# Two additions of a Trainium2 transformer block moved to accumulating DMAs on GpSimd

## The chip, the cores and the metric

The kernel runs on one core of one Trainium2 chip. The core has five engines that work side by side: TensorE (PE, matrix products into PSUM), VectorE (DVE), ScalarE (ACT), GpSimd (POOL) and SyncE (SP), which here only issues DMAs. The metric is the device time of one execution in microseconds. The kernel before took 204.91 us in the median of three runs (204.67 to 206.53).

## The reference

One block of a transformer with 2048 positions of 512 features, in bf16: a layer norm with a condition's scale and shift, local attention with 32 heads over 8 positions (every second one, back to 14 positions before), a residual; then a second layer norm with scale and shift, and an MLP that mixes positions (not features), behind a layer norm of its own.

```python
mod = (_silu(c) @ w_mod).reshape(c.shape[0], 6, 1, -1)
sa, ca, ga, sb, cb, gb = (mod[:, i] for i in range(6))
h = _layernorm(x) * (1 + ca) + sa
x = x + ga * _A_ref(h, A_wqkv, A_wo)            # attention over s, s-2, ..., s-14
h = _layernorm(x) * (1 + cb) + sb
x = x + gb * _B_ref(h, B_w1, B_b1, B_w2, B_b2)
...
def _B_ref(x, w1, b1, w2, b2):                   # mixes the 2048 positions
    h = _layernorm(x)
    u = _gelu(jnp.einsum('bsd,sf->bdf', h, w1) + b1)
    return jnp.einsum('bdf,fs->bds', u, w2).transpose(0, 2, 1) + b2
```

Where a line above shortens the original, it keeps what is computed: the shift row that this document speaks of is `sb`, the scale row is `1 + cb`, and the residual is the first `x + ga * ...`.

## The kernel before

The 2048 positions are 16 tiles of 128 positions by 512 features. `xx` holds them all in SBUF. Attention runs over five chunks of 2, 4, 4, 4 and 2 tiles (`SIZES`). For each chunk there are these steps, by the names that the order uses (the numbers behind a name are the chunk and a part, or the tile):

- `ln1s`, `ln1v`, `rstd1`, `nb1`, `n1`: statistics and normalisation of the input tile, into `h3`. Statistics may be taken by VectorE (`:d`, two instructions) or by ScalarE (`:a`, two passes with an accumulator, and then a small VectorE column `ln1v`).
- `tr`/`hT` or `xt`: the transpose, by TensorE or by a DMA. `qkv` and `ev`: the projections and their evictions from PSUM.
- `qk`: VectorE multiplies q with k shifted by 0 to 14 positions, four instructions of 128x4096 per chunk (128x2048 for the short first and last chunk); `red`: TensorE adds up the heads' features into `psL`.
- `max`, `sub`, `exp`, `esum`, `rcp`, `smB`: the softmax.
- `vd` and `a2`: DMAs that lay out v and the weights; `pv`: VectorE's products of both; `pvacc`, `oev`: their sums and eviction.
- `wo`: the output projection of a tile, four matmuls and a fifth of `xx` with the identity that adds the residual in PSUM; `x1`: ScalarE evicts the sum into `xx` and collects its mean. For tiles 14 and 15 VectorE adds the residual in `x1` itself (`:d`), and the fifth matmul is left out.
- `ln2q` (ScalarE, sum of squares), `ln2m`, `rstd2`, `nb2`, `n2`: the second norm, into `h2`. `aff`: VectorE multiplies by the scale row and adds the shift row, two instructions over one, two or four tiles (`GRP`).
- `ln3s`, `ln3v`, `rstd3`, `nb3`, `h3`: the MLP's norm of `h2`, into `h3`.

The MLP's first product `mlp1` takes tiles of `h3` as they come: a group of its matmuls needs four neighbouring tiles, the first group tiles 0 to 3. Its sums are parked in `gT` (`park`), later ones are added (`padd`) and go through `gelu`. The second product `mlp2` needs all of `gT`; `fin` adds bias and residual and `st_out` stores.

What runs when is written out by hand: the string `ORDER` (L182) lists every step once, and `schedule` (L87) walks it. Each engine executes its own instructions in that order and waits for what they need. A suffix picks the engine or form: `:d` VectorE, `:a` ScalarE, `:p` GpSimd (for `warm`, done on TensorE, where `:s` leaves it out), `:q` a matmul cut into four quarter matmuls of 32 output rows. `warm` are matmuls of the identity whose result nobody reads. All DMAs but one are issued by SP, in the order of the list; each of them waits on SP's queue for what it needs, and those behind it wait with it.

The lines that the change touches are the residual and second norm in `build_chunk` (L798 to L855):

```python
                if res:
                    mm(ps(s_), lhsT=ident[:], rhs=xx[:, st, :], start=False, stop=True)
...
                nc.scalar.activation(xx[:, st, :], ps(s_), ACT.Identity, **acc)
...
        hv = h2[:, g0 - t0:g0 - t0 + gn, :]
        nc.vector.tensor_tensor(hv, hv, ab_bc[:].unsqueeze(1).to_broadcast([P, gn, D]), op=ALU.mult)
        nc.vector.tensor_tensor(hv, hv, sb_bc[:].unsqueeze(1).to_broadcast([P, gn, D]), op=ALU.add)
```

Of the kernel before, what the change touches and what calls it, by code (L numbers as in the profile page):

```python
# [161 lines left out]
def _t_tt2(n):  # L162
    return 0.154 + 0.00052 * n
# [14 lines left out]
def _t_mm(cols, n=1):  # L178
    return n * (cols / 2400.0 + 0.0024)
# [3 lines left out]
ident ld_x0 act_table ld_wmod1 ld_c cps ln1s0:d ln1v0 silu_exp silu_dve ld_x1 ln1s1:d ln1v1 ld_x_1_2 ln1s2:d warm0:p  # L183
rstd1_0 consts halo0 ld_x_1_4 nb1_0 n1_1:p ln1s4:d ld_wmod0 ln1s3:d ln1s5:a ln1v2 ln1v5 ln1v3 ln1v4 ld_x_3_12 rstd1_1
nb1_1 n1_4:d n1_3:a modcols1 modcols0 a1col n1_0:p tr0_0 hT0_2:a hT0_3:a ld_x_2_8 n1_2:p n1_5:d hT0_1:a tr1_2 tr1_0
sab ld_wqkv0 wsc0_3:p qvb0 ln1s8:d ln1s9:a ld_wqkv1 ln1s13:d hT0_0:d qkv0_00 qkv0_10 wsc0_1:p hT1_3:d hT1_1:a hT1_2:d
wsc0_0:p ln1s12:d ln1v9 wsc0_2:a ld_x_2_6 qvb_cp0 ev0_00:a ln1s6:d ev0_10:a qkv0_12 ln1s7:d ln1v12 qkv0_02 hT1_0:a
ln1v6 ln1v8 qkv1_10 ev0_12:a ev0_02:a qk0_1 ev1_10:a ld_wo2 ln1v7 ln1v13 rstd1_2 ld_wqkv2 qvb1 wsc1_0:p wsc1_3:p
ld_x_3_10 wsc2_1:a ld_wmod5 qkv1_00 ev1_00:a qk0_0 qk0_3 ld_wo3 nb1_2 n1_8:a qvb_cp1 qkv0_20 ev0_20:a wsc1_2:a ld_b1
qkv0_22 ev0_22:a ld_x_4_14 red0_0 qk0_2 warm5:s red0_1 red0_2 red0_3 ln1s11:d mask ln1s14:a qkv1_01 qkv1_12 ev1_01:a  # L190
ld_wo0 ln1s10:d wsc2_0:p ld_wmod2 qkv1_11 ev1_11:a ld_wmod4 max0 sub0 exp0 n1_6:p xt6 ev1_12:a qkv1_02 qk1_0 n1_9:a
ld_wmod3 esum0 rcp0 ev1_02:a qkv1_03 ln1v11 ev1_03:a ln1v14 qkv1_13 ld_wo1 qk1_1 n1_7:p ln1v10 smB0 qk1_2 vd0_2 xt7
modrow rstd1_3 xt8 xt9 ev1_13:a nb1_3 a2_0_3 qk1_3 qkv1_22 mrows:a ld_row0 a2_0_1 wsc1_1:a qkv1_21 qkv1_20 ln1s15:a
woq_s a2_0_0 halo_v1:a vd0_0 ev1_20:a wsc2_3:a ln1v15 red1_0 red1_1 red1_2 red1_3 max1 a2_0_2 n1_13:a pv0_2 qkv2_01:q
n1_12:p vd0_1 qkv1_23:q ld_row1 ev1_22:a wsc2_2:a n1_10:a sub1:q vd0_3 xt10 exp1 ev2_01:a pv0_1 qkv2_10:q ev2_10:a
pv0_0 qkv2_11:q pvacc0_2 xt13 pv0_3 esum1 rcp1 smB1 a2_1_3 ev2_11:a qkv2_00 pvacc0_0 qkv2_02:q pvacc0_3 ev1_23:a
ev1_21:a vd1_2 qkv2_03:q qk2_1 a2_1_2 pvacc0_1 vd1_3 oev0_2:a ev2_00:a qkv2_12 halo_v2:a oev0_0:a qk2_0 ev2_02:a wo0
qkv2_13 ev2_12:a qk2_2 qkv2_21 n1_11:a qkv2_22 ev2_13:a a2_1_1 rstd1_4 nb1_4 ev2_03:a qk2_3 xt12 n1_14:a wo1 x1_1:a
red2_0 ln2q1 qkv2_23 ev2_23:a qkv2_20 a2_1_0 xt11 qkv3_01 pv1_2 x1_0:a ln2q0 ln2m0 red2_1 ev2_22:a vd1_0 pv1_0 qkv3_02
red2_2 red2_3 ev3_01:a ev2_20:a ev3_02:a ld_row2 qkv3_11 rstd2_0 ev3_11:a qkv3_13 max2 vd1_1 nb2_0 n2_0:a ev2_21:a  # L200
vd2_3 sub2 xt14 pv1_3 pvacc1_2 exp2 pv1_1 qkv3_10:q qkv3_12:q esum2 n2_1:a ev3_12:a qkv3_00 rcp2 vd2_2 ev3_13:a ld_b2
ev3_00:a oev1_2:a smB2 a2_2_0 pvacc1_1 oev1_1:a pvacc1_3 ld_w1_0_896 oev1_3:a pvacc1_0 qkv3_03 halo_v3:a oev1_0:a wo3
ld_w1_0_512 a2_2_3 wo2 aff0 qk3_2 a2_2_2 ev3_10:a ln3s1:a ln3s0:a qk3_1 ev3_03:a qkv3_23 warm3:s a2_2_1 x1_2:a x1_3:a
ln2q2 ln3v1 ln2q3 ln3v0 qk3_0 warm1:s ev3_23:a vd2_0 wo4 x1_4:a n1_15:p wo5 qkv3_20 biascols ev3_20:a ln2q4 red3_0
x1_5:a pv2_2 xt15 qkv4_00 ln2q5 ln2m2 rstd2_2 rstd3_0 pvacc2_2 qk3_3 nb3_0 ev4_00:a h3_1:a red3_1 qkv4_22 qkv4_12
nb2_2 n2_2:a biascols_cp:a vd2_1 pv2_1 ev4_22:a red3_2 red3_3 n2_3:p oev2_2:a ev4_12:a ln2m4 max3 qkv3_21 warm4:p
warm2:s aff2 qkv3_22 sub3 ev3_21:a exp3 ld_w1_0_0 pv2_0 pv2_3 qkv4_20 h3_0:p ev3_22:a rstd2_4 nb2_4 n2_4:p esum3 rcp3
qkv4_02 ln3s3:d ev4_20:a pvacc2_1 oev2_1:a halo_v4:a pvacc2_0 oev2_0:a n2_5:d ln3s2:a qkv4_10 pvacc2_3 oev2_3:a
ev4_10:a ln3v3 ln3v2 rstd3_2 aff4 nb3_2 smB3 wo7 ev4_02:a h3_3:p wo8 x1_7:a wo9 vd3_3 wo6 ln3s5:d h3_2:a mlp1_0_4_0
mlp1_0_0_0 ld_w2_3 vd3_1 ln3s4:a x1_6:a qk4_1 x1_8:a ln3v5 qk4_0 red4_0 ln3v4 rstd3_4 qk4_3 a2_3_3 a2_3_1 vd3_0  # L210
mlp1_0_2_0:q x1_9:a a2_3_2 red4_1 ln2q9 mlp1_0_3_0:q qk4_2 red4_2 nb3_4 ln2q7 h3_4:a red4_3 a2_3_0 pv3_1 h3_5:a
mlp1_0_1_0:q mlp1_0_1_4:q vd3_2 max4 mlp1_0_0_4:q mlp1_0_3_4:q pvacc3_1 mlp1_0_2_4:q ln2q8 vd4_3 ln2q6 sub4:q
park0_0:a park0_1:a oev3_1:a mlp1_0_4_4:q mlp1_0_6_0:q vd4_0 park0_2:a park0_3:a ld_w1_0_1152 pv3_0 pvacc3_0
mlp1_0_5_0:q exp4 park0_4:a oev3_0:a ln2m6 rstd2_6 pv3_2 mlp1_0_5_4:q park0_5:a nb2_6 n2_6:a n2_9:a pv3_3 mlp1_0_8_0:q
pvacc3_2 ld_w2_4 mlp1_0_7_0:q mlp1_0_9_0:q n2_8:a pvacc3_3 oev3_2:a vd4_1 oev3_3:a n2_7:p mlp1_0_6_4:q esum4
ld_w1_0_1408 aff6 rcp4 park0_6:a smB4 a2_4_1 ln3s7:d wo13 ln3s8:d ln3s9:d ln3v8 ln3s6:d x1_13:a ln2q13 wo10 x1_10:a
ln2q10 wo11 x1_11:a wo12 ln3v7 x1_12:a ln2q12 ln3v9 ln3v6 rstd3_6 nb3_6 a2_4_3 mlp1_0_10_0 mlp1_0_12_0:q a2_4_2 ln2m10
h3_6:d ln2m12 a2_4_0 ld_w2_1 h3_7:a pv4_1 rstd2_10 nb2_10 mlp1_0_11_0:q h3_9:p mlp1_0_12_4:q ln2q11 ln2m11 h3_8:a
n2_10:a pv4_3 ld_row3 rstd2_12 nb2_12 rstd2_11 mlp1_0_8_4:q mlp1_0_7_4:q mlp1_0_7_8:q park0_7:a aff10 mlp1_0_10_4:q
mlp1_0_10_8:q pv4_0 vd4_2 pv4_2 nb2_11 mlp1_0_8_8:q ld_w1_0_1664 ln3s10:a park0_8:a mlp1_0_9_4:q mlp1_0_9_8:q  # L220
ld_w1_1_0 park0_9:a ln2m13 n2_11:p ln3v10 pvacc4_0 pvacc4_1 oev4_0:d mlp1_0_12_8:q pvacc4_2 n2_12:a pvacc4_3 aff12
mlp1_0_11_4 mlp1_0_11_8 aff11 oev4_2:a wo15 x1_15:d rstd2_13 nb2_13 wo14 rstd3_10 nb3_10 mlp1_0_13_0 ld_w1_1_640
x1_14:d ln2s14:d mlp1_0_13_4 h3_10:p ln2v14 n2_13:p aff13 park0_10:a park0_11:a ln3s11:a ln3v11 ln2s15:a rstd2_14
nb2_14 n2_14:p mlp1_0_13_8 ln2v15 ln3s12:d rstd2_15 park0_12:a park0_13:a mlp1_1_0_6 mlp1_1_0_10 mlp1_1_1_6 mlp1_1_4_6
rstd3_11 mlp1_1_4_10 nb2_15 aff14 ln3s14:d ln3v14 mlp1_1_2_6 mlp1_1_2_10 ln3s13:a n2_15:p rstd3_14 nb3_11 ln3v12 aff15
ln3s15:d rstd3_12 nb3_12 ln3v13 rstd3_13 ln3v15 mlp1_1_6_6 nb3_14 mlp1_1_1_10 padd1_0 rstd3_15 mlp1_1_5_6 mlp1_1_5_10
padd1_1 nb3_13 h3_14:p mlp1_1_6_10 mlp1_1_3_6 nb3_15 h3_15:p h3_11:d padd1_2 h3_12:a ld_w1_1_896 mlp1_1_3_10 h3_13:a
mlp1_1_7_10 mlp1_1_10_10 padd1_3 padd1_4 padd1_5 padd1_6 padd1_10 ld_w2_5 mlp1_1_8_10 padd1_8 gelu8 mlp1_1_9_10
padd1_9 gelu9 padd1_7 gelu7 ld_w1_2_0 mlp1_2_1_11 mlp1_2_0_11 mlp1_2_1_14 ld_w2_2 mlp1_2_0_14 padd2_0 gelu0
mlp1_2_2_11 mlp1_2_2_14 padd2_2 gelu2 padd2_1 gelu1 ld_w1_2_640 mlp1_2_3_11 mlp1_2_4_11 mlp1_2_3_14 mlp1_2_4_14  # L230
padd2_3 gelu3 ld_w1_1_1408 mlp1_2_5_11 mlp1_2_5_14 padd2_4 gelu4 padd2_5 gelu5 mlp1_2_6_11 gelu10 padd2_6 gelu6
ld_w2_0 mlp1_1_11_10 padd1_11 mlp1_1_12_10 mlp1_1_13_10 padd1_13 mlp2_0_0 gelu11 mlp2_0_0b ld_w2_15 gelu13 padd1_12
gelu12 mlp2_5_0 ld_w2_7 mlp2_0_0c fin0_0 mlp2_6_0 ld_w2_9 ld_w2_11 mlp2_4_0 mlp2_8_0 st_out0_0 fin4_0 mlp2_2_0
ld_w2_13 st_out4_0 fin8_0 mlp2_1_0 fin1_0 st_out1_0 mlp2_3_0 fin3_0 st_out3_0 fin2_0 st_out8_0 mlp2_7_0 mlp2_12_0
mlp2_9_0 mlp2_13_0 st_out2_0 fin5_0 fin7_0 st_out7_0 fin12_0 st_out5_0 fin6_0 st_out6_0 fin9_0 mlp2_11_0 st_out9_0
fin13_0 fin11_0 st_out11_0 mlp2_10_0 mlp2_14_0 fin10_0 mlp2_15_0 st_out10_0 fin14_0 st_out14_0 fin15_0 st_out13_0
st_out15_0 mlp2_15_1 st_out12_0 fin15_1 mlp2_15_2 fin15_2 st_out15_1 st_out15_2
# [4 lines left out]
def kernel(  # L242
# [15 lines left out]
    NPRE=6,  # L258
    NBIG=4,
    NVD: int = 5,  # L260
    NHT: int = 2,
    NA2: int = 2,
    NB=2,
    NH2=2,
    ESD=(4,),
    LN2D=(14, 15),
    GRP=(2, 2, 4, 1, 1),
    XDMA=(2, 3, 4),
    INJ=(),
    WARM=(48, 24, 16, 16, 8, 8),  # L270
):
    nc = _OrderedNC(tc, 1)
    G = _Graph(dict(ps=6, big=NBIG, vd=NVD))
    CM = max(SIZES) * P
    MT = max(SIZES)
    NCH = len(SIZES)
    T0 = [sum(SIZES[:i]) for i in range(NCH + 1)]

    x_view = A_x[0].rearrange("(t p) d -> p t d", p=P)
    out_flat = out[0]  # L280
    w1_view = B_w1.rearrange("(t p) f -> p t f", p=P)
    w2_view = B_w2.rearrange("(t p) s -> p t s", p=P)
# [722 lines left out]
```

## Time and profile before

| | us |
|---|---|
| three runs, median (lowest to highest) | 204.91 (204.67 to 206.53) |
| the profiled execution, its own time | 205.73 |
| its span, first to last instruction | 203.9 |
| TensorE busy | 190.8 |
| VectorE busy | 159.7 |
| ScalarE busy | 129.6 |
| GpSimd busy | 31.2 |
| mean granted TensorE clock | 0.973 |

The profiled execution's time is 1.83 us longer than its span: what lies before its first and after its last instruction. All operations pass through one recording helper, so every instruction carries its line, L133; they are told apart by the names of the tiles they write and read (`out<-in`). In the lists, a row gives engine, operation, tiles, shape, count, busy time in us and mean ns of one, and after the bar the engine's idle time just before and what ended it. In the timeline, a row begins with start and duration in us, and neighbours of one kind are merged.

Names of tiles: `big` products of q·k and of weights·v, `psS` and `psL` PSUM, `h` any of `h2` and `h3` (buffer numbers are left out), `wst` MLP weights, `rows_bc` the four rows of the condition, spread over the partitions, `mv`, `rs`, `nb`, `sums` columns of the norms.

### The profile page before, as it was taken

Reading aid. Unit: us, or ns where it says so; the run is one execution under the profiler, and the core shown is the slowest. Engines: PE = TensorE matmul, PEld = TensorE weight load, DVE = VectorE, ACT = ScalarE, POOL = GpSimd, SP = SyncE. Lnnn points to the kernel's source line nnn. Section 1 sums busy time; section 2 is a strip of 40 time slices with the busy share of each in tenths; the row PEclk is TensorE's granted clock in tenths of the full one; section 3 lists DMA queues with packets and bytes.
Section 4 is the critical chain, followed back from the end, with each engine's and each line's share of the span. In section 5 each row is a group of like instructions: output and inputs, shape, how many; then the busy total and the mean of one; then the engine's idle time right before and its main releaser. Section 6 shows DMA issues by size and latency. Waiting matters only on the chain.

```text
span 203.9 us, 4231 instructions
## 1 busy us (share of the span) xinstructions
PE 190.8 (94%) x1643; PEld 99.2 (49%) x1643; DVE 159.7 (78%) x244; ACT 129.6 (64%) x311; POOL 31.2 (15%) x50
## 2 busy tenths in 40 slices
PE   5389999999999979989999999999999999999993
PEld 5377654454344436634454464444444444444453
DVE  2687999999999989999999898996741241696554
ACT  2396999987979999899999999873642000000000
POOL 4263403100500006030040103330000000000000
PEclk9856999999999999999999999999999999999999
DMA  5999686649727993267495647789999340022013
GB/s 167 340 325 296 191 199 128 213 55 264 197 80 247 270 309 103 92 197 230 166 264 141 141 121 226 200 249 221 240 297 281 97 136 3 26 97 83 0 55 105
DMA packets 55369, 35.94 MB, mean 176 GB/s; under 512 B 24628, under 2 KB 52788, under 8 KB 55348
## 3 DMA queue, kind: packets, MB, share of 16 engines
q1 hardware_dynamic: 55340, 35.66, 63.3%
q8 instruction: 13, 0.21, 0.5%
q14 instruction: 8, 0.07, 0.1%
q10 hardware_dynamic: 8, 0.00, 0.0%
HBM read 22.03 MB, written 2.10 MB: 118 GB/s over the span
## 4 chain that ended last, share of the span: by engine, by line
PE 60%; DVE 18%; DMA 8%; ACT 5%; SPq 5%; issue 2%; POOL 0%; DVEq 0%
PE psS L133 58%; DVE big L133 8%; SPq L133 5%; DMA a2sb<-lsb 4%; DVE h L133 3%; DMA xx<-in_A_x_dram 3%; DVE st L133 2%; PE psL L133 2%; DVE m L133 2%; DVE mv L133 1%; DMA rows_bc<-mrows 1%; ACT xx L133 1%; ACT junk L133 1%; DVE lsb L133 1%; ACT q_sb L133 1%
## 5 line engine op out<-in xcount | busy, mean ns | idle before, releaser
L133 PEld LDWEIGHTS <-wst 128*32 128x32 bf16 (+1 forms) x626 | 37.2, 101 | 33.0 <-issue 1.6
L133 PE MATMUL psS<-h,wst 128*32 128x512 bf16 (+1 forms) x476 | 51.3, 379 | 0.1
L133 DVE TENSOR_TENSOR big<-a2sb,vD 128x4096 bf16<-128x4096 bf16 (+1 forms) x20 | 37.0, 1876 | 0.8 <-PE psS L133 0.5
L133 DVE TENSOR_TENSOR big<-q_sb,k_f 128x4096 bf16<-128x4096 bf16 (+1 forms) x20 | 36.6, 1858 | 1.3 <-POOL w_qkv L133 1.0
L133 POOL TENSOR_SCALAR h<-xx,rs,nb 128x512 bf16<-128x512 bf16 x14 | 19.7, 1409 | 85.2 <-DVE nb L133 62.0
L133 PE MATMUL psS<-hT,w_qkv 128*32 128x512 bf16 (+2 forms) x228 | 29.9, 358 | 1.3 <-ACT v_sb L133 1.3
L133 DVE SCALAR_TENSOR_TENSOR h<-psS,bcol,rows_bc 128x512 f32<-128x512 f32 (+2 forms) x18 | 12.4, 691 | 23.5 <-PE psS L133 18.3
L133 PEld LDWEIGHTS <-w_qkv 128*128 128x128 bf16 (+1 forms) x270 | 19.7, 109 | 17.6 <-issue 5.1
L133 PE MATMUL psS<-gT,big 128*128 128x512 bf16 x112 | 25.0, 379 | 0.0
L133 PEld LDWEIGHTS <-big 128*128 128x128 bf16 x144 | 12.0, 98 | 16.5 <-DMA big<-in_w_mod_dram 3.2
L133 PE MATMUL psS<-woq,o_sb 128*128 128x512 bf16 x64 | 16.4, 380 | 0.3 <-ACT o_sb L133 0.3
L133 ACT ACTIVATE junk<-xx 128x512 bf16<-128x512 bf16 x24 | 15.1, 629 | 2.0 <-DMA xx<-in_A_x_dram 1.5
L133 ACT ACTIVATE gT<-psS,bcol 128x512 bf16<-128x512 f32 x14 | 9.1, 687 | 7.9 <-DVE psS L133 7.9
L133 DVE TENSOR_TENSOR psS<-psS,gT 128x512 f32<-128x512 f32 x14 | 9.4, 697 | 5.9 <-PE psS L133 5.9
L133 PE MATMUL psS<-hT,wst 128*128 128x256 bf16 (+1 forms) x64 | 13.3, 372 | 0.0
L133 DVE BATCH_NORM_STATS2 st<-xx 128x6 f32<-128x512 bf16 x13 | 8.9, 681 | 5.4 <-DMA xx<-in_A_x_dram 5.3
L133 ACT ACTIVATE h<-xx,nb,rs 128x512 bf16<-128x512 bf16 x15 | 12.0, 811 | 1.6 <-DVE nb L133 1.5
L133 DVE TENSOR_TENSOR h<-h,rows_bc 128x512 bf16<-128x512 bf16 (+2 forms) x20 | 12.0, 605 | 0.3
L133 ACT ACTIVATE q_sb<-psS,qvb 128x512 bf16<-128x512 f32 (+1 forms) x20 | 11.4, 593 | 1.0 <-PE psS L133 1.0
L133 DVE TENSOR_TENSOR h<-h,xx 128x512 bf16<-128x512 f32 (+2 forms) x18 | 11.4, 633 | 0.7
L133 ACT ACTIVATE v_sb<-psS,qvb 128x512 bf16<-128x512 f32 (+1 forms) x20 | 11.4, 596 | 0.0
L133 PEld LDWEIGHTS <-group 128*32 128x32 bf16 x288 | 6.6, 95 | 9.6 <-issue 3.5
(91 smaller groups left out, 240.4 us busy)
## 6 DMA issues: line engine op xcount, KB each, us to landing
vD<-v_sb SPq DMA_DIRECT2D x12, 524.5 KB, 3.6
big<-in_B_w_dram SPq DMA_DIRECT2D x4, 896.0 KB, 9.1
vD<-v_sb SPq DMA_DIRECT2D x8, 268.5 KB, 2.7
wst<-in_B_w_dram SPq DMA_DIRECT2D x3, 640.0 KB, 4.8
out_dram<-h SPq DMA_DIRECT2D x15, 128.0 KB, 1.7
xx<-in_A_x_dram SPq DMA_DIRECT2D x7, 256.0 KB, 7.0
wst<-in_B_w_dram SPq DMA_DIRECT2D x2, 800.0 KB, 4.7
gT<-in_w_mod_dram SPq DMA_DIRECT2D x3, 512.0 KB, 7.6
```

The source lines that it names most:

```text
L133: r = fn(*a, **k)
```

## The change

Two steps get another way of doing them, and one of these ways is chosen per tile in the order:

- *Residual.* A third form of `wo`/`x1`, suffix `:t`: the identity matmul is left out, ScalarE evicts the projection into the tile's place in `h2`, and a new step `xa` on GpSimd first corrects the sum column by the input's mean and then issues a DMA that adds `h2` to `xx`, SBUF to SBUF. It is chosen for tiles 0, 3 and 10. VectorE adds the residual in `x1` (`:d`) for tiles 13 and 14, where it was 14 and 15.
- *Shift row.* `aff` is cut into `affm` (the multiplication, VectorE) and `affa` (the addition), and `affa` may be a DMA of GpSimd, suffix `:p`, that adds the row to `h2`. It is chosen for `affa0` and `affa4` (two tiles each), `affa11` and `affa12` (one each).

The variance columns `ln2m` are computed with scaled sums (the sign and the division move into ScalarE's logarithm); for a single tile this takes one instruction where there were two. And the whole of `ORDER` is a new list: all steps of the old one are there, but most stand elsewhere, and many have another suffix. For instance, the four `qk4` products and `red4` stand ahead of the first `mlp1`, `h3_0`, `h3_2` and `h3_3` are VectorE's, and 37 steps with `:q` become 18.

```diff
@@ parameters
+    ADDS=(2, 2, 2, 2, 1),
+    RDMA=(1, 1, 1, 1, 0),
@@ ln_rstd
-            nc.scalar.activation(lv[:, sl, 0], var, ACT.Ln, bias=epscol[:, 0:1])
+            nc.scalar.activation(lv[:, sl, 0], var, ACT.Ln, bias=epscol[:, 0:1], scale=1.0 if vreads is None else -1.0 / D ** 2)
@@ build_chunk, residual
+            tmp = h2[:, st - t0, :]
+
+            def fx_t(st=st, s_=s_, acc=acc, tmp=tmp):
+                nc.scalar.activation(tmp, ps(s_), ACT.Identity, **acc)
+
+            def fx_p(st=st, tmp=tmp):
+                nc.gpsimd.tensor_scalar(sums[:, st, 0:1], ln_t["mv", 0][:, st, 0:1], float(D), sums[:, st, 0:1],
+                                        op0=ALU.mult, op1=ALU.add)
+                nc.gpsimd.dma_start(xx[:, st, :], tmp, accum_op=ALU.add)
...
+            x1 = wo_.link = G.add_any([("act", 0.69, fx_a), ("dve", 0.75, fx_d), ("temp", 0.69, fx_t)][:na], frees=s_,
+                      writes=[("xx", st)] + ([] if st in LN2D else [("sum0", st)]) + h2k, name=f"x1_{st}")
+            if na == 3:
+                G.add_any([("dve", 0.0, lambda: None), ("dve", 0.0, lambda: None), ("pool", 1.5, fx_p)], reads=h2k,
+                          writes=[("xx", st), ("sum0", st)], link=x1, name=f"xa{st}")
@@ build_chunk, variance of the second norm
+                    if gn == 1:
+                        nc.vector.scalar_tensor_tensor(mv[:, g0, 1:2], sums[:, g0, 0:1], sums[:, g0, 0:1],
+                                                       sums[:, g0, 1:2], op0=ALU.mult, op1=ALU.subtract)
+                        return
...
@@ build_chunk, scale and shift rows
-                nc.vector.tensor_tensor(hv, hv, ab_bc[:].unsqueeze(1).to_broadcast([P, gn, D]), op=ALU.mult)
-                nc.vector.tensor_tensor(hv, hv, sb_bc[:].unsqueeze(1).to_broadcast([P, gn, D]), op=ALU.add)
...
+            add("dve", _t_tt2(gn * D), lambda hv=hv, bc=bc: nc.vector.tensor_tensor(hv, hv, bc(ab_bc), op=ALU.mult),
+                reads=hk + ["ab_bc"], writes=hk, locks=True, name=f"affm{g0}")
+            G.add_any([("dve", _t_tt2(gn * D), lambda hv=hv, bc=bc: nc.vector.tensor_tensor(hv, hv, bc(sb_bc), op=ALU.add)),
+                       ("pool", 1.3, lambda hv=hv, bc=bc: nc.gpsimd.dma_start(hv, bc(sb_bc), accum_op=ALU.add))][:ADDS[ch]],
+                      reads=hk + ["sb_bc"], writes=hk, locks=True, name=f"affa{g0}")
@@ ORDER, the stretch ahead of the first MLP matmuls
+ev3_20:a affm4 pv2_1 esum3 ln3s1:d n2_2:a ln3v1 n2_3:p halo_v4:a halo_v3:a vd3_0 affa4:p vd3_3 ln3s0:a ln3v0 affm2
+qkv4_10 rcp3 warm3:p rstd3_0 smB3 affa2:d pvacc2_1 qk4_3 pvacc2_3 oev2_3:a ld_w1_0_512 a2_3_3 qkv4_00 oev2_1:a wo6
+ev4_10:a ev4_00:a wo7 qk4_0 ln3s2:a ln3v2 a2_3_1 ln3s4:a wo8 ln3s3:a wo9 qk4_1 red4_0 red4_1 qkv4_20 qk4_2 red4_2
+nb3_0 x1_9:a ln3v3 rstd3_2 red4_3 ln3s5:d ln3v5 nb3_2 ln3v4 h3_0:d h3_2:d h3_1:p x1_8:a xa8 h3_3:d mlp1_0_0_0:q
```

## The prediction

> **What bounds the kernel now.** First the page's busy row, then a table of stages, then the instructions around the place where the stages meet. The page:
>
> ```profile
> PE 190.8 (94%) x1643; PEld 99.2 (49%) x1643; DVE 159.7 (78%) x244; ACT 129.6 (64%) x311; POOL 31.2 (15%) x50
> ```
>
> TensorE looks like the bound, but its busy time counts pipelined matmuls that overlap. The table of stages (columns: stretch, length, busy time and instructions of each engine, granted clock, DMA share, GB/s) gives its pace:
>
> ```profile
> 0.00:18.76 18.76, 12.66 (x142) 11.06 (x143) 11.34 (x36) 9.87 (x24) 9.00 (x33) 0.73 0.94 284
> 18.76:92.90 74.14, 70.49 (x664) 36.70 (x663) 72.32 (x73) 69.14 (x163) 13.20 (x8) 1.00 0.69 182
> ...
> 140.00:190.00 50.00, 50.00 (x233) 22.71 (x232) 25.35 (x37) 9.05 (x14) 0.00 (x0) 1.00 0.50 138
> ```
>
> The last row is the pure MLP: about 232 matmuls of 512 columns in 50 us, 0.2157 us each. I count all matmul columns of the program at that pace (a quarter matmul, 128*32, as a quarter, a floor of 25 ns for tiny ones, warm-ups left out). The kernel needs 176.1 us of TensorE and its span is 203.9, so 27.8 us are lost. The timeline says where:
>
> ```profile
> 92.67 0.38 PE L133 MATMUL psS<-xx,ident 128*128 128x512 bf16 x1
> 92.88 1.89 PE L133 MATMUL psS<-h,wst 128*128 128x512 bf16 x8
> ```
>
> At 92.88 the first MLP matmul starts. Work done by then is 69.7 us, so 23.2 us are already lost. The other 106.4 us take 203.9 - 92.88 = 111.0, so only 4.6 us are lost behind it (3.2 of them after the last matmul). **Before the first MLP matmul TensorE waits for others; after it, it never does.** Who it waits for is in the second row of the table: VectorE is busy 72.32 of 74.14 us, ScalarE 69.14. So two numbers set the time: when the first MLP matmul can start, and how much TensorE work is left then.
>
> **The change, part by part.** The named edits are small. Three tiles (0, 3, 10) lose their identity matmul: 3 x 0.2157 = 0.65 us of TensorE. Their ScalarE eviction stays, at the same 588 ns, into another tile. Four shift-row additions leave VectorE (tiles 0-1 and 4-5 at 688 ns each, 11 and 12 at 460 each): 2.30 us. GpSimd gets three one-column operations and seven DMAs. But the written order is new throughout, and it moves far more than that. Summed over the program by the rows of before, VectorE ends at +0.7 us (171.6 against 170.9 of listed durations, additions moved and all), ScalarE at -0.3, GpSimd loses four tile normalisations. No engine gets lighter by more than 0.7 us; what counts is what stands ahead of the first MLP matmul.
>
> That matmul needs the second normalised input of tiles 0 to 3. Before, VectorE's last instruction for it is the nb column of tiles 2-3:
>
> ```profile
> 18.76 3.55 DVE L133 TENSOR_TENSOR big<-q_sb,k_f 128x2048 bf16<-128x2048 bf16 x3 [0.97 <-POOL w_qkv L133]
> ...
> 90.46 0.15 DVE L133 SCALAR_TENSOR_TENSOR nb<-mv,rs 128x2 f32<-128x2 f32 x1
> ```
>
> From the first q·k product to that column VectorE executes 69 instructions whose rows sum to 74.3 us, in 90.61 - 18.76 = 71.85 us: 0.967 us per listed us, as neighbours overlap a little. After, the stretch runs from the first product to the third normalisation (h3_3 is VectorE's now) and holds 76 instructions, priced by these rows and their like:
>
> ```profile
> L133 DVE TENSOR_TENSOR big<-q_sb,k_f 128x2048 bf16<-128x2048 bf16 x8 | 9.4, 1217 | 1.0 <-POOL w_qkv L133 1.0
> ...
> L133 DVE TENSOR_TENSOR h<-h,rows_bc 128x1024 bf16<-128x1024 bf16 x6 | 4.1, 688 | 0.1
> ...
> L133 DVE TENSOR_SCALAR h<-h,rs,nb 128x512 bf16<-128x512 bf16 x2 | 1.2, 608 | 0.0
> ```
>
> Added: the four products of the last chunk, ahead of it now, 4 x 1.217 = 4.87; three normalisations, 3 x 0.608 = 1.82; four more variance columns, 0.84; one v eviction, 0.69; chunk 3's softmax scaling, 0.69. Gone: two two-tile additions, 1.38; one norm, 0.50; tile statistics, 0.86; small columns, 0.17. Net +6.0, so 80.3 us, times 0.967 = 77.6.
>
> When does VectorE begin? Its first product waits for 24 matmuls of 256 columns. In before 36 of them took 6.59 us (183 ns each, clock 0.56 from 9 to 20 us). The changed order sends 72 warm-ups directly ahead, but puts the first bias columns (0.70), their copy (0.15) and a VectorE eviction (0.69) between. The weights it needs are 2.8 MB down the load queue, as in before (13.8 us). Between 109 ns and 183 ns a matmul this gives 17.9 to 19.7 us; I keep 18.8. So h3_3 ends at 18.8 + 77.6 = 96.4.
>
> ScalarE could hold it up. From 18.8 to the last of its instructions that h3_3 needs, its rows (90.3 - 13.2 = 77.1 listed us before) took 71.3 us with 5.0 idle, so 0.860 busy us per listed one. After, 82.4 listed us stand there, among them three more tile statistics of 1.64: 70.9 us, so it could be done at 89.7, and VectorE asks for it at 94.5. The reserve, 4.8 us, is what it was. The cost is 0 to 1.0 us and I take 0.5. First MLP matmul: **96.9**.
>
> TensorE has then done 70.0 us and 105.4 remain; with the same 4.6 lost behind, the span is 96.9 + 105.4 + 4.6 = 206.9, **+3.0 us**. Fewer quarter matmuls cost nothing by the rows (four take the time of one); six more switches of form at about 0.1 us are inside the rounding. Of the warm-ups, the extra 1.8 us fall where TensorE waits anyway; if that cover is gone, they cost 1.8.
>
> The seven DMAs I cost at nothing, if they land under their cover. No GpSimd DMA is in the trace. Nearest rows: SBUF-to-SBUF copies of 128 and 268 KB land 2.6 and 2.7 us after issue, at worst 5.3; issue takes SP 0.6, and a GpSimd operation beside VectorE's products up to 2.6 (below). So 3.2 to 7.9 us, nearer the first, as most such copies are. What queues behind: ScalarE's square of tile 0 has 7 us of other work between, of tile 3 over 6, of tile 10 only 3.2; VectorE's statistics after the additions have 8, 5.3 and, for tile 11, 3.9; tile 4's, on ScalarE, 9. SP's queue is not passed by them.
>
> The profiled execution took 205.73 us round its span of 203.9. The median, 204.91, is 0.8 lower; +3.0 on it is **207.9 us**.
>
> **The rivals.**
>
> *Not slower: the front starts early.* If 72 warm-ups keep the clock at full, the first product starts at 17.9 (-0.9); if ScalarE costs nothing, -0.5; if the 1.4 us of small gaps behind 92.88 close, up to -1.2 more; and the normalisations, at 0.41 where GpSimd is quiet, -0.6. All together 207.9 - 3.2 = 204.7. For it: clock 0.56 exactly where TensorE sat idle 3.1 us after its warm-ups. Against: VectorE's 80.3 listed us still stand there. It decides once h3_3 ends before 94.
> The Trainium skill, "TensorE: Matmul & The Clock Gate", Part 1, says that the clock opens after some 3.4 us of sustained work and closes again after an idle window; the 0.56 after a 3.1 us gap agrees.
>
> *Slower still: late landings.* GpSimd slows beside VectorE:
>
> ```profile
> 78.32 2.64 POOL L133 TENSOR_SCALAR h<-xx,rs,nb 128x512 bf16<-128x512 bf16 x1 [24.77 <-DVE nb L133]
> 80.95 0.76 POOL L133 TENSOR_SCALAR h<-h,rs,nb 128x512 bf16<-128x512 bf16 x1
> ```
>
> The same work takes 0.76 alone and 2.64 beside a 2.29 us product. If descriptors suffer like this, tile 11's addition lands up to 4.0 us late. VectorE waits in order, with the statistics and norms of tiles 11 to 15 behind it. TensorE needs the last of these at once (136.0 in before), so beyond about 1.5 us it passes on: at 4.0 us, 2.5 more, 210.4.
> The Trainium skill, "SBUF — State Buffer", Who interferes with whom, says that VectorE locks GpSimd out in its two-port modes, copies and tensor_scalar among them, and so starves descriptor writing, while tensor_tensor blocks only GpSimd's reads. By that rule the products would leave the DMAs alone and the sum at 207.9; by the row they may cost up to 2.5 us more. No run here shows it yet.
>
> *The order is neutral.* If the edits alone count and TensorE's losses stay as they are, -0.65: 204.3. For it: engine totals hardly move. Against: the first MLP matmul has no other supplier.
>
> **How the numbers follow.** Forecast 0.52 (own range 206.0 to 210.0), early front 0.20, late landings 0.17, neutral order 0.11. The range 203.5 to 212.0 holds all but the outer parts of the rivals. One per cent, about what a measurement of this kernel can tell from no change, is 202.9 to 207.0. Faster: 0.04 of the early front and 0.06 of the neutral order, 0.10. Within: 0.16 and 0.05 of these and 0.05 of the forecast, 0.26. Slower: the rest, 0.64.
>
> **What would show it.** First psS<-h,wst matmul at about 97 (before 94: the early front); VectorE still above 97% busy from its first product to there; loss behind it still near 4.6; GpSimd DMAs landing within 3 to 5 us, and VectorE idle before st<-h of tile 11 under 1 us. I am wrong if VectorE has finished the four last-chunk products and h3_3 by 93, or if TensorE starves after its first MLP matmul.

## The result and the profile after

| | before | after |
|---|---|---|
| three runs, median (lowest to highest), us | 204.91 (204.67 to 206.53) | 222.62 (220.60 to 223.22) |
| span of the profiled execution, us | 203.9 | 220.6 |
| first q·k product on VectorE, us | 18.76 | 24.71 |
| first MLP matmul, us | 92.88 | 107.36 |
| from there to the end of the span, us | 111.0 | 113.2 |

Medians and ranges, here and below, leave out executions over 1.5% above the fastest of their kernel (two of five of c_first_w512 and five of ten of mix_red0_3).

The kernel became slower: ratio 1.083, 95% interval 1.072 to 1.094. The prediction was 207.9 us, and its range ended at 212.0. Its forecast of the span, 206.9, is missed by 13.7 us, and the three stages share that: the first product is 5.9 us later than the 18.8 I kept, the stretch from it to the first MLP matmul takes 82.65 us instead of 78.1 (4.6 more), and what follows takes 113.24 instead of 110.0 (3.2 more).

The busy row of the page after:

```profile
PE 192.9 (87%) x1474; PEld 98.3 (45%) x1474; DVE 158.4 (72%) x244; ACT 130.2 (59%) x311; POOL 38.8 (18%) x56
```

No engine has lost or gained much work, except GpSimd (31.2 before). So most of the new time is waiting. The table of stages of the changed kernel (stretch, length, busy time and instructions of each engine, granted clock, DMA share, GB/s):

```profile
0.00:24.71 24.71, 12.82 (x177) 12.24 (x177) 11.26 (x38) 13.27 (x32) 7.59 (x32) 1.00 0.83 255
24.71:107.36 82.65, 71.14 (x583) 35.03 (x582) 74.30 (x75) 70.16 (x166) 21.18 (x12) 0.99 0.60 171
```

Before, VectorE was busy 72.32 of 74.14 us in the second stage. Now it is busy 74.30 of 82.65: it is no longer what everybody waits for. The waits say what is. First ScalarE's timeline at the start of the changed kernel (start, duration, engine, line, operation; in brackets the idle time before it and what ended it):

```profile
5.01 0.63 ACT L133 ACTIVATE junk<-xx 128x512 bf16<-128x512 bf16 x1
5.55 0.19 ACT L133 ACTIVATION_READ_ACCUMULATOR junk<-xx 128x1 f32 x1
5.77 0.63 ACT L133 ACTIVATE junk<-xx 128x512 bf16<-128x512 bf16 x1
5.78 0.54 ACTq L133 DMA_DIRECT2D c_t<-in_c_dram  x1
...
11.98 0.17 ACT L133 ACTIVATE ecol<-psS 128x4 f32<-128x4 f32 x1 [5.49 <-PE psS L133]
```

and TensorE's timeline there, with the matmul that waits for it:

```profile
11.77 0.18 PE L133 MATMUL psS<-ident,c_t 4*128 4x4 bf16 x1 [11.77 <-DMA c_t<-in_c_dram]
11.88 6.24 PE L133 MATMUL psS<-ident 128*128 128x128 bf16 x72
```

The load of the condition `c` is the one DMA that ScalarE issues (`ACTq`). In the new list it stands behind two tile statistics of ScalarE (`ln1s3:a`, `ln1s5:a`), which wait for tiles of x. Before, it was issued at 0.83 us and its matmul ran at 2.20:

```profile
0.83 0.54 ACTq L133 DMA_DIRECT2D c_t<-in_c_dram  x1
2.20 0.18 PE L133 MATMUL psS<-ident,c_t 4*128 4x4 bf16 x1 [2.20 <-DMA c_t<-in_c_dram]
```

Now it is issued at 5.78, when the DMA engines are busy with SP's loads (their share is 0.83 in this stage), and it lands 5.94 us after that. TensorE does nothing at all for 11.77 us, ScalarE stands idle 5.49, and VectorE 6.8 behind it. The 72 warm-ups, 6.24 us, stand behind that matmul in TensorE's order, so here they too come only after the load has landed.

Then the place where the stages meet, first in ScalarE's timeline of the changed kernel:

```profile
98.08 0.63 ACT L133 ACTIVATE junk<-h 128x512 bf16<-128x512 bf16 x1
98.61 0.19 ACT L133 ACTIVATION_READ_ACCUMULATOR junk<-h 128x1 f32 x1
102.53 0.63 ACT L133 ACTIVATE junk<-h 128x512 bf16<-128x512 bf16 x1 [3.73 <-DMA h<-rows_bc]
```

In VectorE's timeline:

```profile
105.61 0.22 DVE L133 SCALAR_TENSOR_TENSOR mv<-mv,st 128x1 f32<-128x1 f32 x1 [4.21 <-ACT junk L133]
```

And in TensorE's:

```profile
107.36 1.05 PE L133 MATMUL psS<-h,wst 128*32 128x512 bf16 x8 [4.72 <-ACT lv L133]
```

ScalarE waits 3.73 us for an accumulating DMA: the shift row of tiles 4-5. It wants tile 4's statistics, which the first MLP matmul does not need; but tile 3's, which it does need, stand behind them in ScalarE's order. So VectorE idles 4.21 us and TensorE 4.72. GpSimd's timeline shows when that DMA was issued:

```profile
88.93 5.31 POOL L133 TENSOR_SCALAR h<-xx,rs,nb 128x512 bf16<-128x512 bf16 x1 [7.36 <-DVE nb L133]
94.19 1.20 POOL L133 DMA_DIRECT2D h<-rows_bc  x1
```

VectorE had the tile multiplied at 91.56, but GpSimd was still in a normalisation that took 5.31 us beside VectorE's products, so the DMA went out 2.6 us late. It landed at 102.45, 8.3 us after issue.

Last, what lies behind that, in the table of stages of the changed kernel (the granted clock is the third number from the right):

```profile
108.00:110.00 2.00, 2.00 (x24) 0.86 (x20) 2.00 (x2) 2.00 (x6) 0.77 (x1) 0.50 0.00 0
```

and in VectorE's timeline:

```profile
143.75 0.69 DVE L133 BATCH_NORM_STATS2 st<-h 128x6 f32<-128x512 bf16 x1 [2.90 <-DMA h<-rows_bc]
```

After its idle time TensorE works at a granted clock of 0.50, so part of the wait is paid for a second time (how much, no run isolates); and VectorE waits 2.90 us for the shift row of tile 11, with the statistics and norms of later tiles behind it.

### The profile page after: what moved, and what is told of

It is laid out like the page before. It is cut to its first block, busy times and chain, and to the rows that moved or that the text cites. A ratio compares the mean times of both kernels' runs of the same rounds, so it can differ in the third digit from the quotient of the medians.

```text
span 220.6 us, 3897 instructions
## 1 busy us (share of the span) xinstructions
PE 192.9 (87%) x1474; PEld 98.3 (45%) x1474; DVE 158.4 (72%) x244; ACT 130.2 (59%) x311; POOL 38.8 (18%) x56
## 4 chain that ended last, share of the span: by engine, by line
PE 43%; DVE 21%; DMA 15%; ACT 8%; SPq 6%; issue 6%; DVEq 0%; ACTq 0%
PE psS L133 43%; DVE big L133 13%; DMA h<-rows_bc 7%; SPq L133 6%; DMA a2sb<-lsb 5%; ACT junk L133 3%; DMA c_t<-in_c_dram 3%; DVE h L133 3%; DVE st L133 1%; DMA xx<-in_A_x_dram 1%; ACT h L133 1%; DVE mv L133 1%; DVE m L133 1%; ACT xx L133 1%; DVE lsb L133 1%
## 5 line engine op out<-in xcount | busy, mean ns | idle before, releaser
L133 PE MATMUL psS<-h,wst 128*32 128x512 bf16 (+1 forms) x368 | 53.0, 407 | 5.7 <-ACT lv L133 4.7
L133 PEld LDWEIGHTS <-wst 128*128 128x128 bf16 (+1 forms) x530 | 36.0, 104 | 40.1 <-issue 11.0
L133 DVE TENSOR_TENSOR big<-a2sb,vD 128x4096 bf16<-128x4096 bf16 (+1 forms) x20 | 36.8, 1870 | 3.7 <-DMA a2sb<-lsb 3.7
L133 DVE TENSOR_TENSOR big<-q_sb,k_f 128x4096 bf16<-128x4096 bf16 (+1 forms) x20 | 37.2, 1897 | 0.1
L133 PE MATMUL psS<-hT,w_qkv 128*128 128x512 bf16 (+1 forms) x144 | 29.3, 345 | 0.0
L133 PEld LDWEIGHTS <-w_qkv 128*128 128x128 bf16 x186 | 19.3, 111 | 17.6 <-issue 4.0
L133 DVE SCALAR_TENSOR_TENSOR h<-psS,bcol,rows_bc 128x512 f32<-128x512 f32 (+2 forms) x18 | 12.4, 690 | 18.5 <-PE psS L133 18.1
L133 PE MATMUL psS<-gT,big 128*128 128x512 bf16 x112 | 24.8, 379 | 0.0
L133 POOL TENSOR_SCALAR h<-xx,rs,nb 128x512 bf16<-128x512 bf16 x10 | 12.3, 1238 | 51.3 <-DVE nb L133 38.3
L133 ACT ACTIVATE junk<-xx 128x512 bf16<-128x512 bf16 x30 | 18.9, 629 | 2.3 <-DMA xx<-in_A_x_dram 1.4
L133 PEld LDWEIGHTS <-big 128*128 128x128 bf16 x144 | 12.0, 97 | 13.2
L133 PE MATMUL psS<-woq,o_sb 128*128 128x512 bf16 x64 | 16.3, 380 | 0.7 <-ACT o_sb L133 0.7
L133 DVE TENSOR_TENSOR h<-h,xx 128x512 bf16<-128x512 f32 (+2 forms) x18 | 11.4, 632 | 6.6 <-DMA out_dram<-h 6.2
L133 ACT ACTIVATE h<-xx,nb,rs 128x512 bf16<-128x512 bf16 x20 | 15.7, 811 | 0.4 <-DVE nb L133 0.3
L133 ACT ACTIVATE gT<-psS,bcol 128x512 bf16<-128x512 f32 x14 | 9.0, 685 | 8.4 <-DVE psS L133 8.4
L133 PEld LDWEIGHTS <-group 128*32 128x32 bf16 x288 | 5.9, 95 | 15.9 <-issue 7.9
L133 DVE TENSOR_TENSOR psS<-psS,gT 128x512 f32<-128x512 f32 x14 | 9.3, 695 | 5.2 <-PE psS L133 5.1
L133 PE MATMUL psS<-big,group 128*32 128x512 bf16 (+1 forms) x160 | 9.7, 339 | 3.4 <-DVE big L133 3.4
L133 PE MATMUL psS<-hT,wst 128*128 128x256 bf16 (+2 forms) x76 | 11.7, 336 | 0.1
L133 ACT ACTIVATE q_sb<-psS,qvb 128x512 bf16<-128x512 f32 (+1 forms) x18 | 10.7, 612 | 1.5 <-PE psS L133 1.4
L133 PEld LDWEIGHTS <-ident 128*128 128x128 bf16 (+1 forms) x132 | 10.0, 114 | 3.3 <-issue 1.8
L133 ACT ACTIVATE k_f<-psS 128x512 bf16<-128x512 f32 x16 | 9.3, 591 | 2.2 <-PE psS L133 1.1
```

The source lines that it names most:

```text
L133: r = fn(*a, **k)
```

## The experiments

I had three suspects: the *queue* (the load of `c`), the *landing* (the DMAs of GpSimd land late, above all tiles 4-5) and the *order* (the new list has stalls of its own). The first four kernels take them apart. All share the first edit:

```diff
-... ln1s3:a ld_x_1_4 ln1s4:d ln1s5:a ln1v4 ident ln1v3 ld_x0 ld_c cps
+... act_table ld_c ln1s2:d ... ln1s5:a ln1v4 ident ln1v3 ld_x0 cps
```

**c_first.** The edit above alone.

> Changed kernel with the load of c moved up to stand right behind the first activation of ScalarE, as it did before. Queue theory (c was late because its DMA is issued on ScalarE's queue behind two tile statistics, and lost its place on the DMA engines): first q.k product back from 24.7 to about 18.8, all of it kept, time 222.6 - 5.9 = about 216.7 us (215.5 to 218). Rival (the front is set by the weight loads, or the gain is eaten by the waits behind it): product above 22 or the time above 219.5.

Measured 215.12 us (214.79 to 215.59), 7.5 less than the changed kernel. The first product stands in VectorE's timeline at 17.45:

```profile
17.45 2.36 DVE L133 TENSOR_TENSOR big<-q_sb,k_f 128x2048 bf16<-128x2048 bf16 x2
```

The queue theory holds, and the place of one tiny load was the largest single loss; the gain is 1.6 us more than I expected. The product is even 1.3 us earlier than in the kernel before; the granted clock is 1.00 from 9 to 20 us, where it was 0.56. But the first MLP matmul only comes at 100.4: what followed kept its stalls.

**c_first_add_dve.** The four shift rows go back to VectorE:

```diff
-affa0:p ... affa4:p ... affa11:p ... affa12:p
+affa0:d ... affa4:d ... affa11:d ... affa12:d
```

> As c_first, and the four shift-row additions go back to VectorE. Landing theory (the addition of tiles 4-5 lands 8.3 us after issue and stops ScalarE 3.7 us, that of tile 11 costs some 1.8): 6.4 us gained, 1.3 us of VectorE work put back ahead of the first MLP matmul, about 211.7 us, 5 below c_first. Rival (the DMAs only fill time that VectorE's longer order would take anyway): 216 to 218, no better than c_first.

Measured 209.14 us (208.86 to 210.21): 6.0 less than c_first, though VectorE has 2.3 us more to do. The landing theory had said 5, and holds.

**c_first_res_pe.** The residuals of tiles 0, 3 and 10 go back to TensorE:

```diff
-x1_0:t ... x1_3:t ... x1_10:t
+x1_0:a ... x1_3:a ... x1_10:a
```

> As c_first, and the residuals of tiles 0, 3 and 10 go back to the identity matmul on TensorE; the shift rows stay DMAs. Landing theory (nobody waits for a residual DMA for more than some tenths, and it is the shift rows that land late): within 1 us of c_first, by the matmuls 0.65 longer. Rival (the residual DMAs delay ScalarE's squares, and the shift rows behind them on the same queue): 2 us or more below c_first.

Measured 214.01 us (212.89 to 215.54), 1.1 below c_first, and the runs of the two overlap. ScalarE's two waits for residual DMAs in c_first are 1.1 us together. So the residual DMAs are no large part of it.

**c_first_no_dma.** Both edits: the changed order without any DMA of GpSimd.

```diff
-x1_0:t ... x1_3:t ... affa0:p ... affa4:p ... x1_10:t ... affa11:p ... affa12:p
+x1_0:a ... x1_3:a ... affa0:d ... affa4:d ... x1_10:a ... affa11:d ... affa12:d
```

> As c_first, without any of the seven DMAs: the changed order alone. By the steps of the prediction (77.6 + 1.3 us of VectorE from 18.8, 0.5 for ScalarE, 105.6 of TensorE and 4.6 lost behind): first MLP matmul at about 98.2, span 208.4, median 209.4 to 210.5 us. Rival (the order itself has stalls that the prediction's sum of rows does not hold): 213 or more.

Measured 209.72 us (209.12 to 210.5), first MLP matmul at 98.3, span 208.6. This is what the prediction's own steps give with the shift rows put back, 98.2 and 208.4; the stretch is 0.9 longer than by them, the first product (17.96) 0.8 earlier. c_first_add_dve, which keeps the three residual DMAs, is 0.6 lower; the identity matmuls they replace are 0.65, but the runs of the two overlap. Of the 17.7 us between the changed kernel and the one before, the load of `c` is thus 7.5 and the shift rows 6.0. The 4.2 that are left, from c_first_add_dve to the kernel before, are near the 4.5 that the prediction's steps give for the order with the shift rows on VectorE (208.4 against 203.9).

Which of the shift rows is it, and why do they land late?

**c_first_4dve.** In c_first, tiles 4-5 alone:

```diff
-affm4 ... affa4:p
+affm4 ... affa4:d
```

> c_first (215.1 us) with the shift-row addition of tiles 4-5 alone back on VectorE; those of tiles 0-1, 11 and 12 stay DMAs. Theory (most of the 6.0 us between c_first and c_first_add_dve is the one wait of ScalarE for tiles 4-5, and the low clock after it): about 210.8 us, first MLP matmul at 97 to 98. Rival (the late tiles 11 and 12, which lost TensorE time behind, make half of it or more): 212.5 or more.

Measured 210.51 us (210.13 to 210.92): tiles 4-5 alone make 4.6 of the 6.0 us. The rest, 1.4, is left for tiles 0-1, 11 and 12.

**c_first_w512.** In c_first, SP issued a weight load 0.2 us before that DMA. It is moved up:

```diff
-warm4:s sub2 ld_w1_0_896 exp2 ... ld_w1_0_0 qkv3_10 ... oev2_3:a ld_w1_0_512 a2_3_3
+warm4:s sub2 ld_w1_0_896 exp2 ... ld_w1_0_0 ld_w1_0_512 qkv3_10 ... oev2_3:a a2_3_3
```

> c_first (215.1 us) with one weight load of SP, the one issued beside the addition of tiles 4-5, moved up to stand behind the load before it, about 30 us earlier. Queue theory (the accumulating DMA's packets stood behind that load on the same 16 DMA engines): the addition of tiles 4-5 lands some 4.5 us after issue instead of 8.3, ScalarE waits under 1 us for it instead of 4.1, about 211.5 us. Rival (VectorE's products keep GpSimd from writing the descriptors): it still lands after 7 us or more, and the time stays within 1 us of 215.1.

Measured 210.25 us (209.59 to 211.17), 1.3 below what the queue theory gave. But in the profile, which is of an execution of 213.44 us, the landing was 7.0 us and ScalarE still waited 2.5, as the rival said; no profile shows the landing at 210.25. The DMA view of the 2.63 us between issue and its first packet (4.83 in c_first) shows why:

```profile
DMA  9898499996999896969999799996999969979930
...
q1 hardware_dynamic: 255, 0.98, 98.8%
```

The first line is the busy share of the 16 DMA engines in tenths; the second that all of it is `q1`, the queue of SP's transfers (255 packets, 0.98 MB), and none `q0`, GpSimd's. What was left ahead were two copies of v (524 KB each), which SP issues from 85.48 on, 1.4 us before the DMA; in c_first they stood there too, with the load behind them.

**c_first_quiet.** Those two copies are moved as well:

```diff
-halo_v3:a vd3_0 affa4:p vd3_3 ln3s0:a ... a2_3_3 ... a2_3_1
+halo_v3:a affa4:p ln3s0:a ... a2_3_3 ... a2_3_1 vd3_0 vd3_3
```

> c_first_w512 (211.2 us, the addition of tiles 4-5 still 7.0 us from issue to landing, ScalarE waiting 2.5 us) with two of SP's copies of v moved behind the two small copies that follow them, so that neither a load nor those copies are under way when GpSimd issues. Queue theory (its packets stand behind whatever transfers SP has issued before, a load in c_first, the v copies in c_first_w512): first packet 1.5 us after issue ends or less, landing 4 to 5 us after issue, ScalarE waiting under 0.5 us, 209.5 to 210.5 us. Rival (the packets of an accumulating DMA of 256 KB are slow by themselves, beside VectorE's work): landing above 6 us again, 211 or more.

Measured 210.80 us (210.46 to 211.54), landing 3.70 us after issue, no wait of ScalarE for it, first MLP matmul at 96.7. The median is no lower than that of c_first_w512, so the run shows what delays the landing, and no further gain. The DMA view from issue to landing:

```profile
GB/s 0 0 0 0 0 0 0 0 0 0 0 0 0 0 0 0 0 0 0 110 199 188 210 188 188 199 188 199 177 177 188 188 177 177 116 268 163 174 155 69
...
q0 software_dynamic: 272, 0.26, 45.2%
q1 hardware_dynamic: 265, 0.06, 7.4%
```

Nothing moves in the first 1.78 us, then the 272 packets pass at about 190 GB/s. So the transfer is not slow by itself; in the changed kernel it waited while SP's transfers passed. The same view of the changed kernel, from issue to first packet (4.81 us; packets of both queues, then SP's):

```profile
DMA packets 930, 1.48 MB, mean 307 GB/s; under 512 B 33, under 2 KB 700, under 8 KB 930
...
q1 hardware_dynamic: 929, 1.48, 99.5%
```

1.48 MB of SP's transfers went first. Beside this quick landing, too, VectorE was busy (3.97 of the 4.00 us from 86 to 90). The time, 210.8, is 0.3 over the range I gave it, inside the spread of its runs.

**c_first_quiet_d.** As c_first_quiet, and

```diff
-affa11:p ... affa12:p
+affa11:d ... affa12:d
```

> As c_first_quiet, with the shift rows of tiles 11 and 12 back on VectorE. If those two cost what c_first_4dve (210.5) against c_first_add_dve (209.1) says, 1.4 us: 208.1 to 209.1, no slower than the changed order without any DMA (209.7). Rival (they cost nothing once TensorE is not short of work before): within 0.5 us of c_first_quiet.

Measured 208.92 us (208.71 to 209.29), 1.9 less. So the shift rows of tiles 11 and 12, which land 6.7 and 7.0 us after issue in c_first_quiet (SP issues a weight load of 800 KB just before the first and one of 320 KB between them), cost that much, and with the 4.6 of tiles 4-5 that makes 6.5 for the 6.0 of c_first_add_dve, as near as these medians allow.

That leaves the order, and the prediction's claim that VectorE's list sets the first MLP matmul.

**qk4_late.** From c_first_add_dve, VectorE is relieved of the four products that the prediction priced at 4.87 us:

```diff
-... qk4_3 ... qk4_0 ... qk4_1 red4_0 red4_1 ... qk4_2 red4_2 ... red4_3 ... mlp1_0_0_0:q
+... mlp1_0_0_0:q qk4_3 qk4_0 ... qk4_1 qk4_2 ... mlp1_0_0_4:q red4_0 red4_1 red4_2 red4_3
```

> c_first_add_dve (209.1 us) with the four q.k products of the last chunk, and the matmuls that sum them, moved behind the first MLP matmul. By the prediction's price for the order (4 x 1.217 us of VectorE ahead of that matmul): it starts 4.0 to 4.7 us earlier, at 93 to 94, and the time falls to about 205. Rival (ScalarE, whose reserve was 4.8 us, or the last chunk's softmax, now late, sets the end): the first MLP matmul comes less than 2.5 us earlier, or TensorE gives the gain back behind it; 207.5 or more.

Measured 216.97 us (216.76 to 217.22), 7.8 *more*, and the first MLP matmul at 97.6, where it had been 97.8. My price was wrong. VectorE's timeline shows it waiting where the products had stood:

```profile
92.73 0.22 DVE L133 SCALAR_TENSOR_TENSOR mv<-mv,st 128x1 f32<-128x1 f32 x1 [2.35 <-ACT junk L133]
92.86 0.15 DVE L133 SCALAR_TENSOR_TENSOR nb<-mv,rs 128x2 f32<-128x2 f32 x1
95.80 0.22 DVE L133 SCALAR_TENSOR_TENSOR mv<-mv,st 128x1 f32<-128x1 f32 x1 [2.79 <-ACT junk L133]
```

It waits 2.35 and 2.79 us for ScalarE's statistics of tiles 2 and 3. In c_first_add_dve ScalarE ends them at the same time, and there VectorE waits 0.52 for them: the two engines arrive together. Behind the matmul TensorE then starves for the last chunk: 5.16 us busy from 95 to 105 at a granted clock of 0.68, against 8.82 at 1.00 in c_first_add_dve.

**two_late.** Both suppliers are relieved a little:

```diff
-... ln3s3:a ... qk4_1 ... qk4_2 ... h3_3:d mlp1_0_0_0:q rstd3_4 nb3_4
+affa2:d ln3s3:d ln3v3 ... h3_3:d qk4_1 mlp1_0_0_0:q rstd3_4 nb3_4 qk4_2 ... mlp1_0_0_4:q red4_1 red4_2 red4_3
```

> c_first_add_dve (209.1 us; first MLP matmul at 97.8) with both of its last suppliers relieved: two of the last chunk's four q.k products behind the first MLP matmul (2.35 us of VectorE), and the statistics of tile 3 moved from ScalarE (1.5 us) to VectorE. Theory that both engines are tied (qk4_late freed VectorE of 4.8 us and the matmul did not move, since ScalarE's statistics end at 95.8): first MLP matmul at 95.0 to 95.7, 207 us if TensorE keeps the gain. Rival (something else, such as the output projections, sets it): the matmul stays within 0.7 us of 97.8.

Measured 212.72 us (212.22 to 212.97), first MLP matmul at 96.2. The matmul moves by 1.6, somewhat less than expected, so two tied engines is about right; but the time is 3.6 worse than c_first_add_dve. An earlier first MLP matmul was worth nothing here, with the suppliers of the later ones late instead.

**old_order_edits.** The prediction's rival of the neutral order: the list of the kernel before, with the edits alone.

```diff
-x1_0:a ln2q0 ... aff0 qk3_2 a2_2_2 ev3_10:a ln3s1:a ... x1_3:a ... aff4 ... x1_10:a ... aff12 aff11
+x1_0:t xa0 ln2q0 ... affm0 affa0:p qk3_2 a2_2_2 ev3_10:a ln3s1:a ... x1_3:t xa3 ... affm4 affa4:p ... x1_10:t xa10 ... affm12 affa12:p affm11 affa11:p
```

> The order of the kernel before, kept token for token, with the edits alone: residuals of tiles 0, 3 and 10 and shift rows of tiles 0-1, 4-5, 11 and 12 by accumulating DMAs. Neutral theory (the edits by themselves take 0.65 us of TensorE and 2.3 of VectorE away): 204 to 205. Landing theory (each DMA takes 3 us or more, and in this order ScalarE's square of tiles 0, 3 and 10 and its statistics of tile 1 stand right behind their DMA): ScalarE waits 2 to 3 us each, beyond its reserve of 4.8, and the time is 207 to 211.

Measured 236.02 us (234.04 to 237.53), 30 us slower than before. I expected the direction but at most a fifth of the size. The waits of ScalarE (total, times, longest):

```profile
ACT junk L133 <- DMA xx<-h: 12.7, 3, 5.1
ACT junk L133 <- DMA h<-rows_bc: 12.2, 3, 5.4
```

24.9 us of waiting in six waits, 4.1 each where I had said 2 to 3. I had let a reserve of ScalarE absorb 4.8 of it; in the changed order qk4_late found none. What each wait makes of the 30 us, no run isolates.

**old_covered.** The old list with three shift rows as DMAs (tiles 4-5, 11 and 12) and the readers of tiles 4-5 moved back (shown; those of 11 and 12 stay where they were):

```diff
-aff4 nb3_2 smB3 ... h3_3:p ... vd3_3 wo6 ln3s5:d ... vd3_1 ln3s4:a ... x1_8:a ln3v5
+affm4 nb3_2 smB3 ... h3_3:p affa4:p ... vd3_3 wo6 ... vd3_1 ... x1_8:a ln3s5:d ln3s4:a ln3v5
```

> The order of the kernel before with three shift-row additions as accumulating DMAs (tiles 4-5, 11 and 12), each with its readers moved so far behind it that 4 us or more of other work stands between; residuals as before. Cover theory (a covered DMA costs nothing and frees 1.6 us of VectorE, 0.7 of it ahead of the first MLP matmul): 204 to 205.7, not to be told from before. Rival (the DMA slows the shift copies and loads beside it, or GpSimd's normalisations behind its descriptors): 207 or more.

Measured 215.99 us (215.44 to 217.79). It doesn't test what I meant. The steps that I counted as VectorE's cover, `vd3_3` and `vd3_1`, are DMAs of SP, and GpSimd's norm `h3_3:p` held the issue back until 92.26. VectorE had one product left to do and then waited 5.60 us, and GpSimd's DMA landed 5.07 us after issue.

**mix_qk0_3** and **mix_red0_3.** With `c` first, the changed front is 1.3 us faster than the old one. So I joined that front to the old list, cut behind `qk0_3` (shown) and behind `red0_3`; behind the cut stands what is left, in the order of the kernel before:

```diff
-... qvb_cp0 qkv1_11 ev0_02:d qk0_3 ld_wo0 ln1s10:a ld_wo2 ev0_00:a qk0_2 ...
+... qvb_cp0 qkv1_11 ev0_02:d qk0_3 wsc0_3:p wsc0_1:p ln1s12:d wsc0_2:a ev0_00:a ...
```

> The changed order with c first, up to the first q.k product, and behind it the order of the kernel before, without accumulating DMAs. With c first the first product came at 17.4 to 18.1 us, in before at 18.8. If VectorE's stretch from there is that of before (74.1 us to the first MLP matmul), that matmul comes at 91.5 to 92.3 and the time is 203.4 to 204.3 us. Rival (work that the changed order had not yet done by then, statistics and evictions, is missing and takes the gain): 205 to 207.

> As mix_qk0_3, with the changed order kept up to the last sum of the first chunk's q.k products. Same theory: 203.4 to 204.3 us. Rival: 205 to 207; if it is worse than mix_qk0_3 by over 1 us, the changed order loses between the first product and this point.

Measured 206.82 us (205.47 to 208.08), ratio to the kernel before in the same session 1.002 (0.997 to 1.007), and 207.68 us (206.19 to 208.65), 1.011 (1.007 to 1.016). The first product comes at 17.46 in the first of them, the first MLP matmul at 94.5 instead of 92.9: the lead is gone, and the rival holds. No version here beats the kernel before.

## Why the prediction was wrong

- *TensorE never waits after the first MLP matmul* (4.6 us lost behind): true of the order alone (110.3 us for 105.6 of work in c_first_no_dma, 4.7 lost), false with the DMAs, 7.8. The 3.2 more are tiles 11 and 12 (1.9 by c_first_quiet_d) and, as a rest that no run isolates, some 1.3 of the low clock after TensorE's idle time.
- *VectorE starts at 18.8*: the step that failed most. I followed the 72 warm-ups, the bias columns and the weights down the load queue, and not the load of `c`, which is on another queue, ScalarE's, and had been moved behind two waiting instructions there. It cost 7.3 us (24.71 against 17.45 in c_first), the warm-ups behind it included. All else in the step was better than I had it: the clock stayed full, as the rival of the early front wanted, and the product came at 17.45 rather than 17.9 to 19.7.
- *VectorE's 80.3 listed us at 0.967 each*: the sum came out (stretch with ScalarE's 0.5: 78.1 predicted, 79.2 in c_first_quiet, where the first MLP matmul at 96.7 against 96.9 owes 1.3 to the earlier start). Its reading did not. I said that nothing else is late, with ScalarE done at 89.7 and a reserve of 4.8 us. ScalarE's tile 3 was done at 95.8 in c_first_add_dve. Its busy sum up to there was no larger than I had it (68.6 us from 17.4 on, 70.9 by my count); what I had put at nothing was its waiting, though the row of before had 5.0 of it: 9.8 us here, among them 4.9 for VectorE's variance columns and 2.9 for TensorE. The longest stands in ScalarE's timeline there; VectorE, itself held up 2.35 us by a copy of the weights, works off two products and an addition that stand ahead of the column:

  ```profile
  80.94 0.30 ACT L133 ACTIVATE lv<-mv,epscol 128x2 f32<-128x2 f32 x1 [3.29 <-DVE mv L133]
  ```

  So the two engines hand work to each other and arrive together. Taking 4.87 us from VectorE gained 0.2.
- *Seven DMAs at nothing*: the event and nearly the bounds were there, the choice within them wrong. I bounded the landing at 3.2 to 7.9 us and took the lower part; it was 3.6 to 8.3, by what SP had issued before. The trace of before showed that price already: one of its eight 268 KB copies of v, issued at 101.95 us behind two weight loads, lands 6.84 us after issue, with 1.36 MB moving meanwhile. My "at worst 5.3" is the longest of four 128 KB copies alone. The cover of tiles 4-5, 9 us by my count, was 4.6 in the end (94.19 to 98.80); 2.6 of the missing went to GpSimd's late issue. Price: 4.6 us, and 1.9 for tiles 11 and 12.
- *Late landings* had the right event and the wrong cause. I let GpSimd's descriptors be slowed beside VectorE's products. But its DMA instruction took 0.85 to 1.37 us in every run, and 1.21 wholly inside a product of 2.28 in old_order_edits, as in quiet stretches; what lay between was SP's traffic, as c_first_quiet shows. GpSimd's own arithmetic is slow beside the products: the normalisation took 5.31 us in the changed kernel (0.76 alone), and a one-column operation 3.39 in c_first where a quiet one took 0.27. The Trainium skill, "SBUF — State Buffer", Who interferes with whom, says that a VectorE instruction with two inputs in SBUF contends with a GpSimd instruction that reads SBUF and not with one that only writes; both rows agree.
- *Early front* and *neutral order*: the first was right on the clock and lost its lead later (mix_qk0_3). The second is refuted by old_order_edits, where the edits alone cost 30 us, and by c_first_no_dma, where the order without the DMAs still costs some 4.

## What to carry to other kernels

When a list of work is rewritten, follow every queue that can hold something back, and the smallest transfer on the least used queue first: a DMA issued by a computing engine waits for all that stands ahead of it there. A transfer moved from an engine to the DMA queues is priced more by what has been issued before it than by its size (here 2.7 to 3.7 us free, up to 8.6 in traffic), and it needs that much other work between it and its reader, counted on the reader's own engine. A row sum that gives the right total does not show which engine sets it: take its largest term away and see whether the end moves.

## What the runs showed of the hardware

An accumulating DMA of GpSimd, SBUF to SBUF: its instruction takes 0.85 to 1.17 us for 128 KB, 1.20 to 1.37 for 256. On free DMA engines the first packet comes 1.45 us after the start of the instruction, 1.78 for the larger, and it has landed after 2.69 us (128 KB in old_order_edits) and 3.70 (256 KB in c_first_quiet). Where 0.9 to 2.4 MB of SP's transfers moved while it waited, it landed after 4.3 to 8.6.

Where I looked, the two queues mostly took turns. In the changed kernel GpSimd's packets carry 1 KB in the half microsecond from 98.5, with SP's earlier transfers still passing, and 60 KB in the next, beside 80 of SP's; from 99.5 to 100 they have 98 KB and SP's queue a single packet. The last 7 of the 272 pass between 101 and 102.45 amid SP's next transfers, and from first packet to landing it is 3.45 us there and 1.92 in c_first_quiet. The Trainium skill, "DMA: Bandwidth & Descriptors", Issuing engines are not separate DMA queues, says that all of them end on the same 16 engines and interleave there: the first half agrees, and of the second these stretches show little. Why the first packet waits for SP's earlier transfers stays open.

TensorE's granted clock fell from 1.00 to 0.50 in the midst of its idle time, 102.64 to 107.36 us in the changed kernel: it is 1.00 up to 104.9, 0.50 from 105 on, also for the first 4.34 us of work (107.36 to 111.70), and 1.00 again from 111.8. Before, it fell 1.6 us into a pause of 3.14 (1.00 from 6.83 to 8.40, 0.50 from 8.50 to 9.98), sooner in the pause than in the changed kernel.
